# All loads of weights and of the first batch's mask rows issued by SyncE, and another order of the work

## The chip, the cores and the metric

One Trainium2 chip, one core of it. The metric is device time in microseconds of one execution, as the median of repeated runs; a profile is one more execution, taken with the hardware profiler.

## The reference

Cluster attention, then two feed-forward blocks, everything in float32 except that the weights arrive as float64:

```python
# q, k, v: (B=2, H=8, S=768, D=64); 16 centroids per head
q_assign = np.argmax(np.einsum('bhsd,hcd->bhsc', q_n, c_n), axis=-1)
k_assign = np.argmax(np.einsum('bhsd,hcd->bhsc', k_n, c_n), axis=-1)
mask = q_assign[:, :, :, None] == k_assign[:, :, None, :]
scores = scale * np.matmul(q, k.transpose(0, 1, 3, 2))
scores = np.where(mask, scores, -1000000000.0)
attn = softmax(scores)
x = (attn @ v), as (1536 tokens, 512)
h = x @ w_in                      # 512 x 2048
g = where(h >= 1, h, where(h <= -1, 0, (h + 1) ** 2 / 4))
x = g @ w_out                     # 2048 x 512
h = (x @ w1) * (x @ w2) @ w3      # 512 x 1024, 512 x 1024, 1024 x 1024
return h @ w_out2                 # 1024 x 512
```

## The kernel before

The work is cut into some three thousand small steps, each with a name, an engine, what it needs and which buffers it takes and frees (`add`, `Plan`). The steps run in an order that is written out: the string `ORDER` holds, two letters a step, the step's number and which of its engines does it (`Plan.order`). Engines run their own steps in that order, and wait for each other by semaphores. A DMA is a step of the engine that issues it, in that engine's line of work: "DMA" is SyncE (SP), which does nothing else; ScalarE (ACT) issues DMAs between its activations.

The stages, in the order of time. **Batch 0's attention** (to about 190 us): q, k of a pair of heads are split into a high and a low part by conversions on ACT or DVE (L352 and L354, tiles `k`, `q`, `kq`), L859 makes the scores of 128 queries in `sc`, L867 on VectorE takes the row maximum, L872 on GpSimd scales it, L880 on ACT makes the exponentials, L897 transposes them on TensorE, L968 multiplies by v. Beside it the float64 weights are loaded (`chunk`, load at L1101 into a `w` tile of 512 KB), turned into float32 by L1107 and L1111 on ACT and L1115 and L1121 on DVE, and stored to DRAM (`wd`, L1126) for later; L1169 multiplies w3 by w_out2 beforehand, and its results go through DRAM (`wp`). **Batch 1's attention beside batch 0's feed-forward** (190 to 470 us): the exponentials go through a float16 pair in `phl` (two buffers; L352 or L354 the high part, L357 the low), and SP transposes them by DMA (L927, `pt<-phl`, 46 times); the feed-forward's matmuls are L1239 with weights in `whl`. **Batch 1's feed-forward** (470 us to the end): a seven-product scheme of block matmuls (L1492, L1239) with sums on DVE and GpSimd (L1403, L357).

A weight that has been stored is loaded again into one of four `wf` buffers (L1103 in `chunk`, L1413 in `w_unit`), split into `whl` by L352 or L354 and L357, and used by the matmuls. A float64 load takes one of five `w` buffers at first, later of three, and waits for the L1121 that frees it. In batch 0 the mask rows of each head are copied from a tile `mask` into `kq` by two DMAs of `kq_fill` (L728). All these loads, 152 of weights and 14 of mask rows, stand in ACT's line of work. SP issues the loads of q, k, v, the stores, the transposes and the output. The framework tells DMAs' landings by eight semaphores, taken in turn by the DMAs of both engines in the order of the steps: a DMA waits for the one eight before it.

The mask copies' engine is chosen by the batch, and the weight loads name ACT outright:

```python
    def dma_of(b):
        return nc.sync.dma_start if b else nc.scalar.dma_start
```

Of the kernel before, what the change touches and what calls it, by code (L numbers as in the profile page):

```python
# [13 lines left out]
U32 = mybir.dt.uint32  # L14
# [29 lines left out]
    ",(,4,6&E,*<8<6<F<:<V+|<J<L+e<s<<&I<N%@&K<?,8,:,,,.<@+m,#,%<g,<,0,2,>,L,@,B,D+g,N,P<w=*,X,Z,]&N<e<i,F,R<k<Z<]"
    "<n<`<a<p=:;|<0<2,_,T,H,J,V&>+i+l,a,u,w,y<u<y<|=.=J=#%(,c&P-(-*-,+o<B<Q<R,|-#,e,g=>=,=<=0+q=X&@-.&B-4-6-8=@=B"
    "&M=2=D=i-%-:=5=6+s<q=%=(-0-2-<-@&c-B-D=N=L=P=R&S=U=V=Z=]=_&T=y->>0=k-F-L-X-Z-]-N,m,i=a,l-P=m=o=q=s=d=e>@-R-_"
    ">P=|>#>2&Y-H-u-w,o-e-g>%-J>a,q=8=G=H>(,s>4-a-T-V.(.*-d&Z>6-y=g=v=w>o-|>*>-&b>8>:%*>D&i&V&_>T&k&v>B>F>H&^>K>M"
    "&e.#.%-m-i.4.6.,..?#>s.@-k>e.0.3&o.8.B&m.D&g-o>.>=>>.:?4>R>V>c>q&s.L.N.P.X.<>X>Z.Z%B?(-q>N.F>g>i.R.>?F>u>l>w"
    "?%?*>z?,.H>n>~.T.]._.a.J?V.u.V-s>]/(/4?.?0/*/,.c?i&z(&?@>_/@/B.w?2?B?D&w($(-%,?8&q?y.m?Z?J/.?6?H?X&|((%D/6.y"
    ".|/#/8/:/<?m/%?:?<?>?L?]/D?N?_?k?o?a(..e/0/2?q/>%.%0%2%4%F?P.g?R/F?s/L/N/H/P?c@,@2@#@B?|%6%H/J(*/R@T?T?e?g%J"  # L50
    "%L/X%8%:%</Z.i.k.o?u@%@(@6@4@8/T0(/V/]/_.q.s@:?w@.@0@e/a/c/u@*0*0,@D@F@<@w@X/w@>0./y/|@i@V@g@N%N0406@H@J@L@Z"
    "/m/e@]00%P%R%T@kA.@`@m@o0#0%@|02080:@@@P@b@yA#A%@R@q0@0<0L0>/g/i0XA@AP/k0N0P0B0DA:/o0u0w0yA)@c@s@u0Z0R0F0T/q"
    "0H0KA*A2A0A40|0W0]0_0e0gA6ADAcABA,A<A>0a0cA8As/s1((0(2ARATAFAHAJ1*1,1.1#Ag(4(61416AVAXAe1%AMAiAkA]AZ0mAuAnAp"
    "100i1X1Z12B%Aw0kB,0o181:1@1L(:1N1P1B1D(=(8(>ANA_AaAy(AA|B#1R0q1<1]1T1>1F(B1_B/(E(H(M1e1g(NAqB(B*1H1J1V1a1d0s"
    "1i1kBJ2*2,(F(J2.Bi2022C.B01u1w1y1|(Z(P24(R1m(TBMBO1o2#2%26(V(X2(1q1sB2B4282:2<B6CLCkBkBn2FB82H2>2AD02B2DB>BP"
    "B]B@BBBDC02J2L2O2PC2B:B<BRCNCQB_BbBTBF2T2V2X2ZBHC4C6FLC82]BVD>2cBcBY2eB[2R2_2aBoBq2g2i2kBtC:C<BfBgC>B|C#C&Bu"
    "FPBw2m2oCn3%C@CB3(D2C(CD3*3,CF3436By383.30Fe3:CHCpCKC_CRCT3B3<(_C+CaCWC,3>(hD53D(]32CX3F3@CcCe(bFiD@(c(eG#DL"
    "DZ3H3K2y3P3R3TD#D%CZC]D(3V3LD*3NChCqCs3Y3Z3]CuD,DBD6D:3mD<DOCwD9DQD^Cz3_(jDiG(3a3c3e2qE.3gELD`2s3o(t3q3sDDDG"
# [1699 lines left out]
```

## Time and profile before

| what | us |
|---|---|
| median of 3 runs | 721.11 (721.01 to 721.91) |
| the profiled execution | 723.58 |
| its span, first to last instruction | 721.5 |
| busy in the span: PE, DVE, ACT, POOL | 699.0, 618.2, 468.2, 290.9 |
| mean share of full TensorE clock | 0.998 |

The span is the stretch between the first and the last instruction; the rest of the profiled execution lies around it. Busy time of an engine leaves out what its sequencer does: waiting, and issuing DMAs.

### The profile page before, as it was taken

What the parts mean: (1) busy time and instruction counts of PE and PEld (TensorE: products, weight loads), DVE (VectorE), ACT (ScalarE), POOL (GpSimd) and SP (SyncE); (2) the same over time, 40 slices, a digit from 0 to 9 for tenths busy, and PEclk for the clock granted to TensorE, in tenths of its full rate; (3) what the DMA queues carried; (4) which work ended last, traced back from release to release, by engine and by line L of the source; (5) the groups of instructions that cost most, each with busy time, mean ns of one, the idle gap of its engine ahead of it and who ended that gap; (6) DMA issues with size and microseconds to landing.
All of it is one profiled execution on the core that took longest, in us unless ns stands there. A gap on an engine that the chain in (4) does not pass through costs nothing.

```text
span 721.5 us, 11974 instructions
## 1 busy us (share of the span) xinstructions
PE 699.0 (97%) x4173; PEld 631.2 (87%) x4173; DVE 618.2 (86%) x1080; ACT 468.2 (65%) x872; POOL 290.9 (40%) x359
## 2 busy tenths in 40 slices
PE   5999999999999999999999989999999999999998
PEld 2876776677799999999899988999999999999997
DVE  7999999989889998898999879568878869999940
ACT  7998999779786877977787656236764525543211
POOL 3344433221253454455321312317573426387510
PEclk9999999999999999999999999999999999999999
DMA  8357867777989998998989898673222122121122
GB/s 313 124 179 232 278 208 251 249 250 219 231 190 199 216 226 220 215 243 160 267 216 247 208 155 202 155 219 113 59 88 74 45 73 61 52 80 59 58 70 77
DMA packets 125644, 122.36 MB, mean 170 GB/s; under 512 B 83792, under 2 KB 92432, under 8 KB 125584
## 3 DMA queue, kind: packets, MB, share of 16 engines
q1 hardware_dynamic: 103024, 62.18, 36.2%
q10 hardware_dynamic: 22560, 59.42, 26.3%
q8 instruction: 33, 0.54, 0.3%
q14 instruction: 27, 0.22, 0.1%
HBM read 75.79 MB, written 22.28 MB: 136 GB/s over the span
## 4 chain that ended last, share of the span: by engine, by line
PE 71%; DVE 11%; DMA 7%; ACT 6%; issue 3%; POOL 1%; ACTq 0%; SPq 0%; DVEq 0%; POOLq 0%
PE mo L1239 33%; PE sc L1239 6%; PE sc L859 6%; PE sc L1492 6%; PE mo L1492 4%; PE mo L1169 3%; PE av L976 3%; PE sc L897 2%; PE av L968 2%; DMA pt<-phl 2%; PE av L1239 2%; DMA wf<-wp 2%; PE av L1492 1%; DVE tv L1403 1%; ACT P L880 1%
## 5 line engine op out<-in xcount | busy, mean ns | idle before, releaser
L1239 PE MATMUL mo<-X,whl 128*128 128x384 f32 x912 | 167.9, 338 | 0.0
L1239 PEld LDWEIGHTS mo<-X,whl 128*128 128x128 f32 x912 | 159.5, 189 | 1.7 <-DVE G L354 0.3
L1239 PE MATMUL mo<-G,whl 128*128 128x384 f32 x672 | 124.1, 339 | 0.0
L357 POOL TENSOR_TENSOR whl<-wf,whl 128x512 fp32r<-128x512 f32 x62 | 81.2, 1310 | 97.9 <-DVE whl L354 42.2
L1239 PEld LDWEIGHTS mo<-G,whl 128*128 128x128 f32 x672 | 118.2, 188 | 1.0 <-issue 0.6
L867 DVE TENSOR_REDUCE nm<-sc 128x1 f32<-128x768 f32 x96 | 90.0, 950 | 5.7 <-PE sc L859 5.2
L872 POOL TENSOR_SCALAR nm<-nm 128x1 f32<-128x1 f32 x96 | 34.6, 360 | 146.9 <-DVE nm L867 141.5
L352 ACT ACTIVATE whl<-wf 128x512 fp32r<-128x512 f32 x71 | 44.4, 627 | 46.0 <-PE mo L1239 26.2
L1111 ACT ACTIVATE w<-w,down 128x512 uint32<-128x512 uint32 x72 | 54.5, 763 | 8.4 <-DMA pt<-phl 3.9
L859 PE MATMUL sc<-k,q 128*128 128x512 f32 (+1 forms) x192 | 54.1, 363 | 5.7 <-DVE phl L357 2.6
L880 ACT ACTIVATE sc<-sc,nm 128x768 f32<-128x768 f32 x46 | 40.0, 870 | 20.6 <-POOL nm L872 19.8
L1115 DVE SCALAR_TENSOR_TENSOR wf<-wf,w 128x512 uint32<-128x512 uint32 x72 | 51.0, 714 | 2.3 <-ACT wf L1107 1.7
L1107 ACT ACTIVATE wf<-w 128x512 f32<-128x512 f32 x72 | 47.4, 671 | 6.3 <-POOL whl L357 3.6
L1121 DVE SCALAR_TENSOR_TENSOR wf<-w,wf 128x512 uint32<-128x512 uint32 x72 | 50.3, 702 | 1.1
L880 ACT ACTIVATE P<-sc,nm 128x768 f32<-128x768 f32 x50 | 44.8, 898 | 9.9 <-DVE nm L867 5.6
L859 PE MATMUL sc<-kq 80*128 80x512 f32 (+1 forms) x192 | 49.7, 341 | 0.0
L357 DVE TENSOR_TENSOR phl<-sc,phl 128x768 f16<-128x768 f32 x46 | 43.8, 952 | 3.2 <-ACT phl L352 2.6
L357 DVE TENSOR_TENSOR whl<-wf,whl 128x512 fp32r<-128x512 f32 x50 | 35.1, 704 | 10.1 <-ACT whl L352 9.4
L859 PEld LDWEIGHTS sc<-k,q 128*128 128x128 f32 x192 | 31.4, 190 | 13.5 <-ACT pt L352 4.2
L897 PEld LDWEIGHTS sc<-ident,P 128*128 128x128 f32 x300 | 33.5, 140 | 10.1 <-ACT P L880 7.2
L1239 PE MATMUL sc<-G,whl 128*128 128x384 f32 x228 | 42.0, 339 | 0.0
L897 PE MATMUL sc<-ident,P 128*128 128x128 f32 x300 | 39.7, 275 | 2.3 <-ACT P L880 2.1
(235 smaller groups left out, 1462.0 us busy)
## 6 DMA issues: line engine op xcount, KB each, us to landing
wf<-wd ACTq DMA_DIRECT2D x64, 256.0 KB, 2.8
w<-in_w_out_dram ACTq DMA_DIRECT2D x24, 512.0 KB, 4.2
wd<-wf SPq DMA_DIRECT2D x48, 256.0 KB, 3.4
...
```

Of the source, the lines that this page charges most:

```text
L352: nc.scalar.activation(out=out, in_=in_, func=AF.Copy)
L357: (nc.gpsimd if e == "POOL" else nc.vector).tensor_tensor(out=out, in0=a, in1=b, op=ALU.subtract)
L859: nc.tensor.matmul(ps[:, n], q[0:n_rows, q0:q0 + 128], k[0:n_rows, n], start=first, stop=not first)
L867: nc.vector.tensor_reduce(out=nm, in_=T[("sc", b), s], axis=AX.X, op=ALU.max, negate=True)
L880: nc.scalar.activation(out=new(("P", b), s).rearrange("p n s -> p (n s)") if by_pe(s) else T[("sc", b), s], in_=T[("sc", b), s], func=AF.E ...
L897: nc.tensor.transpose(T[("sc", b), s][:, c], p[:, c], ident)
L1107: nc.scalar.activation(out=T["wf", i], in_=T[w64, i].bitcast(F32)[:, :, 1], func=AF.Abs, scale=float(2.0 ** -112))
L1111: nc.scalar.activation(out=lo, in_=lo, func=AF.Identity, scale=float(2.0 ** -29 - 2.0 ** -41), bias=down)
L1115: nc.vector.scalar_tensor_tensor(out=w, in0=w, scalar=3, in1=T[w64, i][:, :, 0], op0=ALU.logical_shift_left, op1=ALU.bitwise_or)
L1121: nc.vector.scalar_tensor_tensor(out=w, in0=T[w64, i][:, :, 1], scalar=0x80000000, in1=w, op0=ALU.bitwise_and, op1=ALU.bitwise_or)
L1239: nc.tensor.matmul(acc, w[:, a, k4 * 128:(k4 + 1) * 128], rhs(c, k4), start=(first and k4 == 0 and n == 0), stop=(last and k4 == 3 and n = ...
L1492: nc.tensor.matmul(ps, lhs(av, a, k), rhs(bv, c, k), start=k == 0 and n == 0, stop=k == 1 and n == 2,)
```

## The change

The steps that load weights, and those that copy batch 0's mask rows, are now steps of SP. What each loads, and where it lands, stays. `ORDER` is another string of the same steps; in it some steps that can run on two engines stand on the other one. The diff, of `ORDER` its first line:

```diff
-    "###*#,#0#%#(#8$V%X%[#.#2#4$0$.$6$2$X%e%h$8$:#F%V%b$<%c%q%k%m$Z$_$a%i%]$>$c$4$H#D$J#R#g%y&,:m:|%_#Z$%$(;0;>$@"
+    "###%#*#,#0#.#(#8#<$V%X%[$.%e%i$0%c%q#2#4$6%h%m$8$:$2$X#T#F#Z%V%b$_$<%_$a%y&,$Z$4#_$H#D$>$@$c$J%]$e$L%k$B$g$N"
...
-    def dma_of(b):
-        return nc.sync.dma_start if b else nc.scalar.dma_start
+    def dma_of(e):
+        return nc.sync.dma_start if e == "DMA" else nc.scalar.dma_start
...
-            dma = dma_of(b)
+            dma = dma_of(e)
...
-                    ("k2", u, h), {"DMA": 1.95} if b else {"ACT": 0.3}, p - 6.0, kq_fill(u, h),
+                    ("k2", u, h), {"DMA": 1.95} if b else {"DMA": 0.9}, p - 6.0, kq_fill(u, h),
...
-                nc.scalar.dma_start(out=new(w64, i), in_=src.bitcast(U32).rearrange("p (n t) -> p n t", t=2))
+                (nc.sync if e == "DMA" else nc.scalar).dma_start(out=new(w64, i), in_=src.bitcast(U32).rearrange("p (n t) -> p n t", t=2))
             else:
-                nc.scalar.dma_start(out=new("wf", i), in_=src)
+                (nc.sync if e == "DMA" else nc.scalar).dma_start(out=new("wf", i), in_=src)
...
-            add(("wl", i), {"ACT": 0.2}, t - 14.0, load, list(needs) + W_AFTER[i:i + 1], [(w64, i)], behind="w64", moves=((0.46, 1.8),))
+            add(("wl", i), {"DMA": 0.5}, t - 14.0, load, list(needs) + W_AFTER[i:i + 1], [(w64, i)], behind="w64", moves=((0.46, 1.8),))
...
-            add(("wl", i), {"ACT": 0.2}, t - 12.0, load, needs, [("wf", i)], behind="wf", moves=((0.46, 1.05),))
+            add(("wl", i), {"DMA": 0.5}, t - 12.0, load, needs, [("wf", i)], behind="wf", moves=((0.46, 1.05),))
...
-                nc.scalar.dma_start(out=new("wf", i), in_=wd[n])
-
-            add(("wl", i), {"ACT": 0.2}, t - 16.0, load, [("wd", n)], [("wf", i)], behind="wf", moves=((0.46, 1.05),))
+                (nc.sync if e == "DMA" else nc.scalar).dma_start(out=new("wf", i), in_=wd[n])
+
+            add(("wl", i), {"DMA": 0.5}, t - 16.0, load, [("wd", n)], [("wf", i)], behind="wf", moves=((0.46, 1.05),))
```

What this moves is shown at three places, where a name's number tells a buffer.

**SP, about 415 to 445 us**, in the last third of batch 1's attention: DMA transposes `pt<-phl`, stores `wd<-wf` and `xd<-tmp`. Before:

```order
L927 DMA_TRANSPOSE pt_97<-phl_112 128x12x128
L1017 DMA xd<-tmp 128x384
L927 DMA_TRANSPOSE pt_98<-phl_111 128x12x128
L1126 DMA wd<-wf 128x512
L927 DMA_TRANSPOSE pt_98<-phl_112 128x12x128
L1126 DMA wd<-wf 128x512 x2
L927 DMA_TRANSPOSE pt_96<-phl_111 128x12x128
```

and now, with the loads `w<-in_w_dram` among them:

```order
L927 DMA_TRANSPOSE pt_97<-phl_112 128x12x128
L1017 DMA xd<-tmp 128x384
L1101 DMA w_115<-in_w_dram 128x1024
L1126 DMA wd<-wf 128x512
L927 DMA_TRANSPOSE pt_98<-phl_111 128x12x128
L927 DMA_TRANSPOSE pt_98<-phl_112 128x12x128
L1101 DMA w_113<-in_w_dram 128x1024
L1126 DMA wd<-wf 128x512
L1101 DMA w_114<-in_w_dram 128x1024
L1126 DMA wd<-wf 128x512
L927 DMA_TRANSPOSE pt_96<-phl_111 128x12x128
```

Three loads that stood in ACT's line stand between the transposes, and two of them ahead of the transpose into `pt_96`.

**ACT, from its first mask (`mask_118`, L588) to its first exponential (L880)**, about 15 to 24 us; `w` and `wf` are weights on their way to float32. Before:

```order
L588 ACTIVATE kq_105<-sc_175,nbig 16x384
L728 DMA kq_106<-mask_118 16x2x384 x2
L1107 ACTIVATE wf<-w_114 128x512
L352 ACTIVATE vn<-sc_175 128x768
L1101 DMA w_117<-in_w3T_dram 128x1024
L1111 ACTIVATE w_114<-w_114,down 128x512
```

and now:

```order
L588 ACTIVATE kq_105<-sc_180,nbig 16x384
L1111 ACTIVATE w_113<-w_113,down 128x512
L1107 ACTIVATE wf<-w_114 128x512
L588 ACTIVATE mask_118<-sc_180,nbig 128x384
L352 ACTIVATE vn<-sc_180 128x768
L1111 ACTIVATE w_114<-w_114,down 128x512
L1107 ACTIVATE wf<-w_115 128x512
L1107 ACTIVATE wf<-w_116 128x512
L1111 ACTIVATE w_115<-w_115,down 128x512
```

The mask copies and the load are gone from between the activations, and one more L1107 stands ahead of the first exponential.

**ACT, about 72 to 78 us**, where q and k of a later pair of heads are split. Before:

```order
L1101 DMA w_113<-in_w_out_dram 128x1024
L352 ACTIVATE kq_105<-kq_119 64x768
L1107 ACTIVATE wf<-w_115 128x512
L728 DMA kq_107<-mask_118 16x2x384 x2
L352 ACTIVATE pt_98<-sc_174 128x768
```

and now:

```order
L352 ACTIVATE kq_105<-kq_119 64x768 x2
L1107 ACTIVATE wf<-w_115 128x512
L352 ACTIVATE pt_98<-sc_179 128x768
L352 ACTIVATE whl<-wf 128x512
L1111 ACTIVATE w_117<-w_117,down 128x512
```

One conversion more stands on ACT here, and one less on DVE. Over the program, of batch 0's conversions into `k`, `kq` and `q` ACT has 26 (20 before) and DVE 10 (16 before); GpSimd has four operations fewer than before, of all its work.

## Rows read from the trace of the kernel before

**Rows 1.** The page, part 1: busy us, share of the span, instructions.
```profile
PE 699.0 (97%) x4173; PEld 631.2 (87%) x4173; DVE 618.2 (86%) x1080; ACT 468.2 (65%) x872; POOL 290.9 (40%) x359
```

**Rows 2.** Busy time by stretches: length, busy us (instructions) of each engine, PEclk, DMA, GB/s.
```profile
20.00:50.00 30.00, 28.59 (x192) 23.18 (x191) 28.83 (x47) 28.51 (x51) 11.96 (x18) 1.00 0.45 144
50.00:100.00 50.00, 49.22 (x298) 36.48 (x298) 47.37 (x78) 46.21 (x79) 21.70 (x25) 1.00 0.74 245
100.00:150.00 50.00, 47.68 (x293) 33.21 (x290) 47.02 (x73) 44.55 (x78) 15.56 (x21) 1.00 0.75 246
150.00:200.00 50.00, 48.44 (x279) 37.31 (x278) 45.63 (x72) 39.29 (x70) 11.20 (x22) 1.00 0.84 233
200.00:400.00 200.00, 199.52 (x1242) 187.88 (x1242) 184.44 (x298) 154.18 (x282) 83.88 (x102) 1.00 0.93 218
400.00:470.00 70.00, 67.84 (x422) 63.37 (x417) 53.65 (x88) 33.68 (x61) 19.53 (x25) 0.98 0.81 175
470.00:600.00 130.00, 130.00 (x742) 129.59 (x741) 103.91 (x216) 66.98 (x145) 63.18 (x70) 1.00 0.32 98
600.00:640.00 40.00, 39.01 (x220) 38.35 (x220) 39.03 (x75) 19.96 (x46) 21.64 (x24) 1.00 0.18 53
640.00:685.00 45.00, 44.01 (x247) 42.64 (x247) 43.59 (x89) 14.64 (x36) 32.68 (x39) 1.00 0.21 65
```

**Rows 3.** Timeline of ACT, 56 to 63 us: start, us, engine (ACTq issues), what.
```profile
56.22 0.90 ACT L880 ACTIVATE P<-sc,nm 128x768 f32<-128x768 f32 x1
56.23 0.33 ACTq L1101 DMA_DIRECT2D w<-in_w_in_dram  x1
...
62.79 0.60 ACTq L728 DMA_DIRECT2D kq<-mask  x1
```

**Rows 4.** Chain of waits, 15 to 27 us: start, us, what.
```profile
18.85 0.16 ACTq L728
...
25.56 0.19 ACTq L1101
```

**Rows 5.** Groups: ACT 20:200 us, DVE 50:100, DVE whole; busy us, mean ns | idle before.
```profile
L1107 ACT ACTIVATE wf<-w 128x512 f32<-128x512 f32 x39 | 25.4, 676 | 1.6 <-DMA wd<-wf 1.2 <-issue 0.3
L352 ACT ACTIVATE kq<-kq 64x768 fp32r<-64x768 f32 x5 | 4.2, 841 | 0.1
...
L354 DVE CAST kq<-kq 64x768 fp32r<-64x768 f32 x4 | 2.2, 552 | 0.1
...
L357 DVE TENSOR_TENSOR whl<-wf,whl 128x512 fp32r<-128x512 f32 x50 | 35.1, 704 | 10.1 <-ACT whl L352 9.4
```

**Rows 6.** Chain of waits, 405 to 445 us.
```profile
417.98 12.90 DMA pt<-phl
```

**Rows 7.** Timelines of DVE, ACT, PE, 425 to 436 us; in brackets idle before, releaser.
```profile
430.97 0.96 DVE L354 CAST phl<-sc 128x768 f16<-128x768 f32 x1 [4.22 <-DMA pt<-phl]
...
426.79 4.50 ACTq L1101 DMA_DIRECT2D w<-in_w_dram  x2
431.33 0.75 ACT L1111 ACTIVATE w<-w,down 128x512 uint32<-128x512 uint32 x1 [3.92 <-DMA pt<-phl]
...
432.97 1.01 PE L859 MATMUL sc<-k,q 128*128 128x512 f32 x2 [2.16 <-DVE phl L357]
```

**Rows 8.** Busy time by stretches, columns as in rows 2.
```profile
433.00:437.00 4.00, 4.00 (x15) 3.81 (x16) 3.62 (x6) 2.29 (x5) 1.23 (x2) 0.61 0.89 299
```

**Rows 9.** Landing of the transposes L927: all 46, then those of 415 to 435 us.
```profile
DMA to landing us min/median/max: 3.6/4.2/13.0
...
DMA to landing us min/median/max: 3.7/10.3/13.0
```

**Rows 10.** ACT's timeline, 238 to 262 us: a load, and the split of what it brought.
```profile
240.11 0.33 ACTq L1103 DMA_DIRECT2D wf<-wd  x1
...
251.80 0.63 ACT L352 ACTIVATE whl<-wf 128x512 fp32r<-128x512 f32 x1
```

**Rows 11.** SP's waits ahead of transposes L927, 200 to 400 us: ns min/median/max, first and last start.
```profile
L927 SPq EVENT_SEMAPHORE  x34: 17/17/4611, 201.4 to 396.0; - x34
```

More of the change, by code (lines that the diff above doesn't have):

```diff
@@ L44 @@
[L44 to L58, printed above, removed]
@@ new lines @@
+    "&4*m<%;u+@+#+&+B+<*i*l+0+2+L+N+X;w;X<H<X+D+F+P+R;Z&*+T+H<c&G+Z*o<**r<,<.+>;z&><s+]+_+u+a+e&/&<+g+J+V+d*s,4+w"
+    ",(,*<6<8,6<:<F<J&8<V&I%(<L<<<N&E+y+|<Z;i,,,.+m,8<?<@,:<w,#,%,0,<,2,>&J,@,L,B,D,N,P<g,X,Z,]<]<`<b=*=:<e;k,F,R"
+    ";|<0,_%%=J<2<i<k<n<o=X,T,H,J,V+i+l,a,u,w,y<u<y=.,c<|-(-*=#+o<B<Q=i<R&P,|=N-,=,&@&B,e=0=<=>-.-4-#-6&c+r+s-8,g"
+    "-:=2=5=y&N=7=@=B=D-%=]<q-0-2=L=P-<=%=m=R=Z&R=T-@-B=_-X-L-N->-D-F&L=V>0=k>@-P,i,k&T%@=a-Z-]=(>P=d=e-R&i&u-_>4"
+    "&Z>#,m,o,r-H-u-w=o-K=8=G=q=H=s-a.(.*,s=|>%>D>(&a>a>o>2-T-V-c-y-e-g-|&k&W&_=g=u&e.4.,.#.%-m.6>6=w>8>:&p>+>B&X"
@@ new lines @@
+    ">F>H>-&]>K>L-i-l...0.@.3.B-o?#&s?4%B>T>s&g.8.:>.>=>>.<>R>V>X>c?(>e.L.N>g>q-q.X&m.>>N.D.F.P.R.T?%.Z.]._.H.J.V"
+    "?F%*>Z>u>i?V?*>w>l>y?,.a&q.u.c>]>n?/?0>~-s/4/(/*/,&z&|(&?@/@&w?6?J?8?i.w.y/B>_(.?2?B?D?Z(#(-%,/.()%D.m?m?H?X"
+    ".|/#/6/8/:/</0?:?<?>?k/%/2/>?y@2?]?L?o?_?N?P?c.e.g?q%.%0%2%4%F/D/F/L/N/H%H?R?T@B@#/J?s?a@T@,@6/P/R?u%6%8?e?g"
+    "%:%<@e%J%L/T.i.k/X/Z.o/V?|@%@4@8?w@.@0@(@*@:/]/_/a.q.s@F/c@D@X@<@>0(/u0*/w/y0406%N/|@wA.(*@H0,0./m@J@V@L@N%P"
+    "%R/e%T000#@Z@g@i@k080:@|0%02A@@]@`@a@m@o@y@@@P@q@RA#AP(40<0@0L0>A:0N0X/g/i/k0B0u0Z0P0R0D0FA%A(0w0]0_A*0yA2/o"
@@ new lines @@
+    "/qADA0AB@c@s@uAcAs0T0H0K0WA40a0cAT0|AFAHA,A<A>0e0gA6/sARAV1((0(2(61*1,AKA8AXAZ1#141%AM1618Ag1.0mAeAiAkAnAoA]"
+    "AwAuB,10121X1ZB%0i0k0o1L1@1N1BAN1:1<(:(=A_AyA|(8(>AaB#1P1R1T(A1>(D(C(M1D1F1]1_1e1g(N0qAqB(B*1H1a1J1V1d1iBJ(H"
+    "0s(F(ZBi2*2,B.B02.201u1w1y1|(P(R2324BL1k1m1o1r1s(T(VC.(JBNBlBm2#2%2(26(X282:CLCkB2D0B4B7B8B;B>B@2<BBBD2F2H2J"
+    "B=2>2@2BC0C32D2L2NB]B_BP2P2RFLD>2T2VBaBFBRBcBHCNBTBVCQBe2XC4C62c2eBYB[2Z2]2_2aBoBqC8C:C=BsBu2gBg2i2kDLB|C#3%"
+    "3(3*2m2oCmC&C?BxByC(3,C@CBCDCFC_3436D2D4C*CoCa3.30(]CcDZCeCg383:3<32CRCTDACICjCKDi2q3>3@Cq3B3DC-CVCX3FFeD#G#"
@@ new lines @@
+    "D%D)3H3J2s3P3R3T3V3L3NDND*DCC[CsCuDQCwFPE.2y3_D,D:3Y3Z3]Fi(aD63aD.(_3c3m3o(c(eC]3e3gD=(jD83i3kD]DD3qDF3s(s(k"
+    "DHDJ(h3u3w3|D_(uELDVDX2u2wDkDRDTCy(o2|4#3y(mDm404244E046483#4>(w4@4B4%4)(qE3EkF04DDeDaENDgEP4:4<4G4HF>C|D|4L"
+    "4N4PE#DcE%FN)(FRFTDo4JFVEnEoDqDsE(E+Du4RE,4U4V4X4ZE@4]EBEEDwDyFgEFFkEIFmFoE4E6E8E:4_E_EaEd4aEK4*5:GLE<E>4c4e"
+    "EeG(F2F5Gu4g(y(|)#)%4,4.G%EgG*G,HDEiERF@F#F%F)ETEVGP5<5>EX5@F*FBEqEsEvFYFZ4i4k4m5BGN5D5FG.F6F8GRGyGwEwG|E[GT"
+    "H#H%F,F:F<Fq4o4qHHHm4w4y4|4s4uFHF/FDFs5#G1G3FJF])*HF5%HJ5(5H5JGVI,5*FFF_HLIDHoEyFa5VHq5L5N5P5,Hs5RGXG@GBGEHu"
@@ new lines @@
+    "Hw5TFcHN5X5ZG[FuGFE]).),5e5gFw5])5FyF|5`5a5cE|)1)25iI.5.I0I2IHH(I4I]IuGIGJG]G_GaGiGk5kGcGm5s5u5nGoGfH*5oG450"
+    "52G6G8G:5wGgHPHSHyI6IF5y5|G=545658IJ6#IL6(6*G>H|5qI_GqGsH8H:IaJDIcIyH<H>)6Iw6%)AI|H,H.H0H2INJ#J%6,6.HTHVHXH4"
+    "60)9IeI8I:)<HaHc6R6THZ62HeI(I*H7IPHg)BJmISI#6V6X6ZJFJH64);)>IjIkHjK46D6]6FHAJJI%JL66I<I>KTIgHCI@6H6JJ(H]6a6c"
+    "JqJoJsJu)DIX6L6N6_6e6g6iKuIT6PHk6k6mJPJRKXIBK6JNIZJ+)FK868K:IVK<6>)HJw)J)LK>6o6q6s7#Im7%H`Io7(KVKZK]6u6w6y6|"
+    "K_)NL<LTJTJVJYJZKwJ,J.J0J2IqJzJ|72Is74767*KyJ]J_J4J7K|7,7.J8J:J<J>JAK@70KCL#6:Ja7N787:7<7>JcJf6<6@7PJgJjJlJB"
@@ new lines @@
+    "KDKFKIKJ7RL@K#K%KaL>Kc7]7_7TK(K*LB7VKLKN7a7cKPLV7e7@7XK,K.LD7gL(L*KeKgLXK0Lu)P7Z7iLyLwKRLZKiLHL]L|7k7m7o7H6B"
+    "L%M4L_MTM#K27y7|LJLF)TKk7q7sL,L.KmMm7u7w8#8%L1L2M%8(8*8,Lb8<8>M8L4L6M(KoKqKsL8L:)VLL7B8@8BM6M:MV8.M<M>LN7D7F"
+    "807JLcLPLeMXMZMqMoM]M*LSM,M@)_N482NLLg)S)]8486)X88LmMb)cLi8DM.MBMD)hMs)a)e8F7L8:LoM_LlMdMu)[8HN6NmNNMLM08JMF"
+    "8X8Z8]M2MNMyM~MHMKMeN8N:8g8i8kMPMi8_8aNPLqLsMhN<8c8LNR8m8oN@NT8qN,N>)iMSNB8e8sNYNZ)k)mMwN#8R9*9,9.N%O,OLMkNq"
+    "N.NH)o)q)sNoNsN)NuNV9092N0N*8uNe948w8yNyN~NJ96O0O.NgNjOPNDO2O4NF988N8PN39:9<O9NlOeP,O:8|9#ONO#O%Nw9%9(OROTN]"
@@ L96 @@
+    "f#fifgf%hHf(gwgyh&g|fmh*gVgLgFgXhhh$fofqfZfkgTgJh<hJfshjh.h3gZh,hoh>hLi(h7h0hqfufwgPgagNg_hBhNg]giglh8h(hsgc"
+    "gmh4hmi+i,h@hFhDhkhThXhPhRgfgghVh_i.i0hZh]hui2i4hbhch|i6i>i8iDiNiaiFiHiPi#idhxi@ifiLiJiihyiSiTigi%iWiBi:i<ik"
+    "iXiniZi]i_ioiqisiuiwiyi|"
 )
```

64 lines of the change are left out of this document (23 added, 41 removed).

## The prediction

> **What bounds the kernel now.** Begin with the page's busy times: TensorE is busy for 699.0 of the span's 721.5 us [rows 1]. What the change can win is therefore inside 22.5 us of idle TensorE time, plus what a lowered clock costs. Neither the matmuls nor their number change. Next read the busy times by stretches for where those 22.5 us lie [rows 2]. From 20 to 200 us TensorE lacks 1.41, 0.78, 2.32 and 1.56 us, 6.07 together, and there VectorE is busy for 28.83 + 47.37 + 47.02 + 45.63 = 168.85 of 180 us, ScalarE for 158.56. From 200 to 400 us it lacks 0.48, from 400 to 470 us 2.16, from 470 to 600 us nothing, from 600 to 640 and from 640 to 685 us 0.99 each, with VectorE busy for 39.03 of 40 and 43.59 of 45. The remaining 12 are the first 20 us, when there is nothing to multiply, and the tail. So three places can be argued about: the attention of batch 0, where VectorE and ScalarE together set the pace; one hole between 400 and 470 us; and the VectorE-bound stretch from 600 us.
>
> Then the chain of waits. Its one large link that a DMA makes is at 417.98 us: a transpose that takes 12.90 us to land [rows 6]. The timelines after it show what hangs on it [rows 7]: VectorE's next `phl` conversion (L354) waits 4.22 us for it, ScalarE's L1111 at 431.33 idles 3.92, and TensorE's scores 2.16, which is all that TensorE lacks in that stretch. After this hole the granted clock from 433 to 437 us is 0.61 [rows 8], between its levels of 2.4 and 1.2 GHz.
>
> **The change, part by part.** The sum is made against the profiled execution: 723.58, of which 721.5 are the span. It lies 2.47 above the median of 721.11, so the sum's differences are taken from the median at the end.
>
> *ScalarE's issuing.* 166 DMA issues leave ScalarE. A load's issue takes 0.33 us, a mask copy's 0.60 [rows 3]: 152 x 0.33 + 14 x 0.60 = 58.6 us. That looks like a tenth of ScalarE's 468.2, but it lies beside work: the load issued at 56.23 runs under an exponential that began at 56.22 and ends at 57.12 [rows 3]; the sequencer issues while the engine computes. On the chain of waits from 15 to 27 us, where ScalarE has most to do, three such issues of about 0.2 us stand, the first 0.16 and the last 0.19 [rows 4]. They go, about 0.5 us. In return one more L1107 stands ahead of the first exponential, 0.68 us [rows 5]. Both ends: 0.5 gained, or 0.7 - 0.2 = 0.5 lost; I take **0**.
>
> *Conversions from VectorE to ScalarE in batch 0.* Six more of the 36 conversions of q and k are on ScalarE: 0.84 us each there, 0.55 on VectorE [rows 5]. VectorE loses 6 x 0.55 = 3.3 us, ScalarE gains 6 x 0.84 = 5.0. Upper end: the two engines hold up all that TensorE lacks there, and better balance gives back all 6.07. Lower end: ScalarE gets the whole 5.0 us in its busiest stretch, 50 to 100 us, where it is busy for 46.21 of 50 [rows 2]: 51.2 us of work in 50, 1.2 lost. VectorE has 180 - 168.85 = 11.15 us idle and yet TensorE waits, so its load is only part of the cause. I take the nearest measured thing, the waits in the two busier VectorE stretches, 20 to 100 us, 1.41 + 0.78 = 2.19, and halve it as VectorE is one of two engines that set the pace: **1.0 gained**.
>
> *The hole at 418 to 437 us.* The two loads that ScalarE issues at 426.79 take its sequencer 4.50 us, and L1111 stands behind them [rows 7]; the transpose of 417.98 travels beside weight loads. In the changed order ScalarE has no load to wait with, so 3.92 us of idle ScalarE go. Whether TensorE gains depends on the transpose itself: those between 415 and 435 us take 10.3 us in the middle, all 46 take 4.2 [rows 9]. If its loads go one after another in SP's line, at most one or two of them share the DMA engines with a transpose, and it lands nearer 4.2 than 12.9; `phl` is free 8.7 us earlier, and the 4.22 us of VectorE wait go, with the 2.16 of TensorE. At 0.61 granted clock four microseconds do the work of 2.44, so the fall costs 4 x 0.39 = 1.56. Upper end: 2.16 + 1.56 = 3.7. Lower end: the same stall moves, 0 gained. I take **3.0**, nearer to the upper end, because only transposes in that stretch are so slow.
>
> *From 600 us.* GpSimd has four operations fewer. If VectorE takes all four between 600 and 685 us, at the 0.70 us of its L357 [rows 5], it has 2.8 us more to do, where 0.97 + 1.41 = 2.38 are free [rows 2]: 0.4 lost at worst. At best TensorE's 0.99 + 0.99 = 2.0 close. The order moves as much to as away from VectorE, so **0**. From 470 to 600 us VectorE is busy for 103.91 of 130 and covers any such change; without that cover each operation would cost its 0.7.
>
> *SP's line.* It takes 166 more DMAs. At ScalarE's prices these are 58.6 us. SP computes nothing, so only order matters: each DMA waits for the one ahead of it in line. A load is issued 11.7 us before the split of what it brought (240.11, 251.80) [rows 10], so a load that stands behind one transpose (4.2 us) is still in time. For transposes it is the other way: a load that waits for a free `w` holds them. SP's waits ahead of a transpose are now 17 ns in the middle and 4.61 us at most [rows 11]. Best: no loss (0). Worst: it costs as much as the present hole, 3.7 us, at two places in batch 1's attention: 7.4 lost. I take **0**, since the middle wait is nothing.
>
> Sum: 0 + 1.0 + 3.0 + 0 + 0 = 4.0 us. The profiled execution would be about 719.6 (span 717.5), the median 721.1 - 4.0 = **717.1**.
>
> **The rivals.** *No change (721).* The hole of 418 us only moves. For it: transposes travel on SP's queue already, and the DMA engines are busy for 0.93 of 200 to 400 us [rows 2]; the same bytes through one queue are the same load. Then the 3.0 go, the balance gives 0 to 1: 720.1 to 721.1. The Trainium skill, page DMA: Bandwidth & Descriptors, section Issuing engines are not separate DMA queues, says that all engines' DMAs end on the same 16 DMA engines, and that issuing from several saves only the time of issuing. By that rule alone this rival is what comes. The trace agrees as to the share of issuing in the chain (0.2 us a time), but shows transposes between 3.6 and 13.0 us, which the rule does not speak of.
>
> *Slower: transposes behind waiting loads (727.5).* In the new order two loads into `w` stand ahead of the transpose into `pt_96`. Each needs a `w` that L1121 has freed. ScalarE's line shows what such a wait is: 4.50 us for two issues at 426.79 [rows 7]. Now it would stand on SP, and the transpose, both `phl` buffers, VectorE's next conversion and TensorE's scores stand behind it, in this order. From 4 us on (the 4.22 that VectorE waited cost TensorE 2.16) it decides. Two such places cost 2 x 3.7 = 7.4, less the 1.0 of the balance: 721.1 + 6.4 = 727.5. For it: that stretch has no spare buffer for `phl`. Against it: an order can put loads behind the L1121 that frees their buffer, and TensorE lacks only 0.48 us in the 200 us before, while SP already waits up to 4.61 there [rows 2, 11]. The Trainium skill says on the same page, section Anatomy of one DMA, that DMA engines do not wait on semaphores; the issuing sequencer does, before it dispatches. By that rule a load that waits holds all that is behind it on SP; the 4.50 us agree.
>
> *Larger gain (710).* If the balance gives all 6.07 and the hole all 3.7, and from 600 us half of 2.0 comes back: 10.8, so 710.3. For it: VectorE is above 94% in 20 to 150 us. Against it: VectorE is relieved by 3.3 us only.
>
> **How the numbers follow.** Forecast (717.1): 0.40. No change: 0.15. Slower: 0.27. Larger gain: 0.18. The sum's bounds alone reach from 0.5 + 6.1 + 3.7 + 2.0 = 12.3 gained (708.8) to 0.5 + 1.2 + 0 + 0.4 + 7.4 = 9.5 lost (730.6). The range takes both rivals with a little beyond each, **709 to 729**, and leaves out less than 2 in 10; the forecast's own range is 714.5 to 719.5. A measurement here tells about 0.2%, 1.4 us, from no change: faster by more is 0.40 + 0.18 = 0.58, within it 0.15, slower 0.27.
>
> **What would show it.** Right: no link of over 6 us from a transpose in the chain around 418 us; the stretch 400 to 470 us with TensorE over 69 of 70 and a granted clock of 1.00; VectorE's sum in 20 to 200 us lower by about 3, ScalarE's higher by about 5, and TensorE's lack there about 5. The balance is wrong if ScalarE's exponentials start later at 24 us, or if TensorE waits longer for ScalarE's `pt` or `P` from 50 to 100 us. The slower rival shows as semaphore waits over 4 us on SP ahead of L1101 with a transpose behind, VectorE waiting there for `pt<-phl`, and a clock under 1.00 after it. If TensorE's idle time between 20 and 200 us shrinks to 2 or less, the larger gain is right.

## The result, and the profile after

| | before | after |
|---|---|---|
| median, us | 721.18 (4 runs, 721.01 to 721.91) | 714.70 (4 runs, 713.85 to 715.5) |
| the profiled execution, and its span | 723.58, 721.5 | 714.0, 712.3 |
| ratio of the times | | 0.9908, 95% interval 0.9891 to 0.9925 |

The change is faster by 6.5 us; 717.1 had been forecast. Busy time by stretches of the new kernel (length, then busy us and instructions of PE, PEld, DVE, ACT and POOL, granted clock, DMA share, GB/s), beside [rows 2, 8]:

```profile
0.00:20.00 20.00, 13.57 (x81) 7.86 (x82) 14.82 (x37) 15.93 (x22) 7.02 (x15) 1.00 0.91 329
20.00:50.00 30.00, 28.03 (x185) 22.14 (x184) 27.11 (x44) 28.38 (x50) 11.94 (x18) 1.00 0.43 136
50.00:100.00 50.00, 48.82 (x293) 36.16 (x293) 45.30 (x71) 48.40 (x84) 20.80 (x26) 1.00 0.69 229
100.00:150.00 50.00, 48.24 (x296) 32.92 (x294) 47.11 (x73) 45.53 (x78) 15.55 (x21) 1.00 0.77 252
150.00:200.00 50.00, 49.33 (x291) 39.35 (x290) 45.67 (x72) 40.01 (x71) 17.23 (x26) 1.00 0.80 231
200.00:400.00 200.00, 199.99 (x1249) 187.92 (x1248) 180.21 (x288) 155.65 (x282) 84.59 (x103) 1.00 0.89 219
400.00:470.00 70.00, 70.00 (x438) 66.52 (x437) 54.62 (x94) 35.60 (x65) 18.70 (x23) 1.00 0.79 198
470.00:600.00 130.00, 130.00 (x741) 129.69 (x740) 112.63 (x234) 69.05 (x151) 57.55 (x68) 1.00 0.27 85
600.00:640.00 40.00, 40.00 (x230) 40.00 (x229) 37.67 (x80) 18.15 (x43) 19.87 (x24) 1.00 0.20 60
640.00:685.00 45.00, 45.00 (x258) 44.85 (x257) 40.43 (x86) 14.33 (x34) 26.35 (x32) 1.00 0.23 71
```

What TensorE lacks in each stretch, as length less busy time:

| us | before | after | |
|---|---|---|---|
| 0 to 20 | 8.25 | 6.43 | -1.8 |
| 20 to 200 | 6.07 | 5.58 | -0.5 |
| 200 to 400 | 0.48 | 0.01 | -0.5 |
| 400 to 470 | 2.16 | 0 | -2.2 |
| 600 to 685 | 1.98 | 0 | -2.0 |
| the rest | 3.6 | 3.8 | +0.2 |

That is 6.7 us of idle time. TensorE's busy time falls by another 2.5 (699.0 to 696.5), 1.56 of it, by the prediction's estimate, in the stretch at a granted clock of 0.61 [rows 8], which is gone. Together they are the 9.2 us between the two spans. The medians differ by less, since the profiled execution of before lay 2.4 us above its median and that of after 0.7 below.

The first two rows of the table are not firm. Three runs below keep the old order and the old queue up to 190 us (the tail, the 12 loads, the later loads on SP): in their profiles TensorE lacks 7.6 to 8.4 us to 20 us and 5.1 to 5.5 from 20 to 200. The new kernel, profiled again, lacks 7.9 and 5.5. So the 0.5 from 20 to 200 us is no gain, and the 1.8 of the first 20 us is not there in every execution.

The page's part 1, and the queue (packets, MB, share of 16 engines), say that all went to one queue and the bytes stayed (62.18 and 59.42 MB on two queues before):

```profile
PE 696.5 (98%) x4172; PEld 630.6 (89%) x4173; DVE 608.6 (85%) x1076; ACT 474.5 (67%) x880; POOL 281.1 (39%) x355
...
q1 hardware_dynamic: 125584, 121.60, 61.0%
```

The landing of all 46 transposes, beside [rows 9], and what hung on it: the chain of waits from 400 to 450 us is TensorE's matmuls alone.

```profile
DMA to landing us min/median/max: 3.6/4.1/8.1
```

```profile
by line: PE mo L1239 80.2%; PE sc L859 12.6%; PE av L976 6.1%; PE mo L954 1.3%
```

How long SP waits is told by the view of its waits, not by how long its semaphore instructions take, as [rows 11] have it: a DMA's own wait is not in those. From 190 to 470 us, ahead of transposes (the longest group) and of weight loads (us in total, times, longest):

```profile
SPq L927 <- DVE wf L1115: 22.3, 5, 7.8
...
SPq L1101 <- DVE wf L1121: 6.2, 6, 2.2
```

What a transpose waits for is its own `phl`: of the 46, the one in the middle leaves 0.03 us after VectorE's L357 has written it (in the kernel before too). The latest leaves 3.7 us after it (before: 1.9), as it stands on SP behind a load that waits for a `w`:

```profile
316.26 0.95 DVE L357 TENSOR_TENSOR phl<-sc,phl 128x768 f16<-128x768 f32 x1
```

```profile
317.37 3.03 SPq L1101 DMA_DIRECT2D w<-in_w_out_dram  x2
...
320.94 2.06 SPq L927 DMA_TRANSPOSE pt<-phl  x1
```

It cost TensorE nothing: from 200 to 400 us it lacks 0.01.

### The profile page after: what moved, and what is told of

Same layout as the page of the kernel before. It is cut to its first block, busy times and chain, and to the rows that moved or that the text cites. A ratio compares the mean times of both kernels' runs of the same rounds, so it can differ in the third digit from the quotient of the medians.

```text
span 712.3 us, 12067 instructions
## 1 busy us (share of the span) xinstructions
PE 696.5 (98%) x4172; PEld 630.6 (89%) x4173; DVE 608.6 (85%) x1076; ACT 474.5 (67%) x880; POOL 281.1 (39%) x355
## 4 chain that ended last, share of the span: by engine, by line
PE 86%; ACT 9%; issue 2%; DVE 2%; DMA 1%; SPq 0%; ACTq 0%; POOL 0%; DVEq 0%
PE mo L1239 40%; PE sc L1492 9%; PE sc L859 8%; PE sc L1239 6%; PE mo L1492 5%; PE av L976 3%; PE mo L1169 3%; PE sc L897 3%; PE av L968 2%; PE av L1492 2%; ACT P L880 2%; ACT pt L352 2%; ACT w L1111 2%; PE av L1239 1%; ACT wf L1107 1%
## 5 line engine op out<-in xcount | busy, mean ns | idle before, releaser
L357 POOL TENSOR_TENSOR whl<-wf,whl 128x512 fp32r<-128x512 f32 x65 | 86.3, 1329 | 125.9 <-DVE whl L354 64.6
L1239 PE MATMUL mo<-G,whl 128*128 128x384 f32 x720 | 133.6, 339 | 0.0
L1239 PEld LDWEIGHTS mo<-G,whl 128*128 128x128 f32 x720 | 126.4, 188 | 1.2 <-issue 0.3
L872 POOL TENSOR_SCALAR nm<-nm 128x1 f32<-128x1 f32 x96 | 30.6, 318 | 131.3 <-DVE nm L867 125.4
L352 ACT ACTIVATE whl<-wf 128x512 fp32r<-128x512 f32 x74 | 46.2, 627 | 38.9 <-PE mo L1239 15.3
L357 POOL TENSOR_TENSOR wh<-ws,wh 128x256 fp32r<-128x256 f32 x47 | 36.1, 782 | 41.0 <-ACT wh L352 26.3
L880 ACT ACTIVATE sc<-sc,nm 128x768 f32<-128x768 f32 x46 | 39.9, 867 | 17.8 <-POOL nm L872 17.5
L1121 DVE SCALAR_TENSOR_TENSOR wf<-w,wf 128x512 uint32<-128x512 uint32 x72 | 50.5, 707 | 1.1
L1107 ACT ACTIVATE wf<-w 128x512 f32<-128x512 f32 x72 | 47.6, 672 | 4.1 <-DMA wd<-wf 2.1
L880 ACT ACTIVATE P<-sc,nm 128x768 f32<-128x768 f32 x50 | 44.6, 895 | 6.9 <-POOL nm L872 3.8
L357 DVE TENSOR_TENSOR phl<-sc,phl 128x768 f16<-128x768 f32 x46 | 43.8, 952 | 5.6 <-ACT phl L352 5.2
L352 ACT ACTIVATE pt<-sc 128x768 f32<-128x768 f32 (+1 forms) x43 | 33.7, 808 | 5.2 <-PE sc L897 3.8
```

The lines of the kernel that those rows point to most:

```text
L352: nc.scalar.activation(out=out, in_=in_, func=AF.Copy)
L357: (nc.gpsimd if e == "POOL" else nc.vector).tensor_tensor(out=out, in0=a, in1=b, op=ALU.subtract)
L880: nc.scalar.activation(out=new(("P", b), s).rearrange("p n s -> p (n s)") if by_pe(s) else T[("sc", b), s], in_=T[("sc", b), s], func=AF.E ...
L1107: nc.scalar.activation(out=T["wf", i], in_=T[w64, i].bitcast(F32)[:, :, 1], func=AF.Abs, scale=float(2.0 ** -112))
L1121: nc.vector.scalar_tensor_tensor(out=w, in0=T[w64, i][:, :, 1], scalar=0x80000000, in1=w, op0=ALU.bitwise_and, op1=ALU.bitwise_or)
L1239: nc.tensor.matmul(acc, w[:, a, k4 * 128:(k4 + 1) * 128], rhs(c, k4), start=(first and k4 == 0 and n == 0), stop=(last and k4 == 3 and n = ...
```

## The experiments

Each was timed in interleaved rounds with the kernel before on the same chip. Three chips were used (runs 1 to 4, 5 to 8, 9 to 12); before's median on them was 721.3, 720.5 and 720.8.

**The new order alone.** The new kernel, loads and copies issued by ScalarE:

```diff
-        return nc.sync.dma_start if e == "DMA" else nc.scalar.dma_start
+        return nc.scalar.dma_start
...
-                (nc.sync if e == "DMA" else nc.scalar).dma_start(out=new(w64, i), in_=src.bitcast(U32).rearrange("p (n t) -> p n t", t=2))
+                nc.scalar.dma_start(out=new(w64, i), in_=src.bitcast(U32).rearrange("p (n t) -> p n t", t=2))
```

(and so for the other two loads). The first line of this edit also puts on ScalarE the 24 copies of batch 1 that SP issues in both kernels, which the expectation does not say; so only batch 0 is read from it.

> The new order, but all loads and mask copies issued by ScalarE again, at their places in that order. If the gain of 6.5 us comes from the order alone (theory O): 714 to 716, ratio 0.990 to 0.993. If it comes from the loads leaving ScalarE's line (theory Q): 719 to 722, with ScalarE waiting for transposes or stores ahead of its loads between 400 and 470 us. If an order made for SP holds ScalarE up at loads that wait for a free w: over 724.

783.37 us, ratio 1.086 (1.082 to 1.090). The third case came, and far beyond its bound. In batch 0 alone TensorE lacks 17.85 us from 20 to 200 us (after: 5.58), with VectorE and ScalarE busy for only 144.70 and 145.30 us, and the granted clock is 0.93:

```profile
20.00:200.00 180.00, 162.15 (x923) 119.85 (x925) 144.70 (x219) 145.30 (x248) 56.02 (x76) 0.93 0.60 200
```

**The old order with all loads on SP.**

```diff
-        return nc.sync.dma_start if b else nc.scalar.dma_start
+        return nc.sync.dma_start
...
-                nc.scalar.dma_start(out=new("wf", i), in_=src)
+                nc.sync.dma_start(out=new("wf", i), in_=src)
```

> The old order, but all loads and mask copies issued by SP. Theory Q: 715 to 718, TensorE without a gap between 400 and 470 us (2.16 before) and a granted clock of 1.00 there. Theory O: 720 to 722, the hole of 418 us stays. If loads that wait for a free w hold the transposes behind them (the slower rival): over 724, with SP waiting over 4 us at loads L1101 and VectorE waiting for pt<-phl.

728.3 us, ratio 1.0098 (1.0064 to 1.0132): slower by 7. The hole is closed as theory Q says, and yet the time is that of the third case. By stretches, of the fastest of its six executions (724.86 us, mean granted clock 0.998; the others have 0.997 to 0.990), so that the trace shows only half of the 7 us:

```profile
0.00:20.00 20.00, 10.53 (x54) 4.51 (x55) 12.85 (x32) 14.27 (x19) 7.01 (x15) 0.96 0.76 283
...
400.00:470.00 70.00, 70.00 (x455) 65.08 (x453) 57.03 (x95) 36.34 (x66) 20.88 (x28) 1.00 0.81 196
...
640.00:685.00 45.00, 42.79 (x238) 41.11 (x238) 43.19 (x85) 14.69 (x36) 32.14 (x39) 1.00 0.23 73
```

The loss begins in SP's timeline: four weight loads stand ahead of a load of q. SP issues it at 8.96 us, when an earlier load of k has landed (8.94), and it lands 9.00 us later (chain of waits). In the kernel before it leaves at 4.75 us and lands 5.0 us earlier. TensorE waits for it:

```profile
4.58 3.76 SPq L1101 DMA_DIRECT2D w<-in_w_out_dram  x4
8.96 0.33 SPq L513 DMA_DIRECT2D kq<-in_qT_dram  x1
```

```profile
2.66 6.28 DMA kq<-in_kT_dram
8.94 0.02 issue
8.96 9.00 DMA kq<-in_qT_dram
```

```profile
18.00 1.25 PE L539 MATMUL sc<-kq,cT 128*32 128x384 f32 x6 [1.91 <-DMA kq<-in_qT_dram]
```

So a line that holds others up behind it is real, but its victims are loads of q and mask copies in batch 0 (another 1.9 us of TensorE's wait is for `kq<-mask`), not transposes: these took at most 5.9 us here.

**The tail and the start of the new order on the kernel before.** Loads stay on ScalarE. The edits of `ORDER` are given in words, here and below.

```diff
-ORDER = (the 3036 steps of before)
+ORDER = (the first 2600 steps of before, then the others as they follow in the new order)
```

> The kernel before with its loads on ScalarE, and from step 2600 of 3036 on (about 600 us) the order and the engine choices of the new kernel. If TensorE's 2.0 us between 600 and 685 us went by the order of that stretch alone: 719.2, with at most 0.3 us of idle TensorE there. If they need the loads on SP: 721, with 1 to 2 us of idle TensorE left.

719.96 us, ratio 0.9977 (0.9952 to 1.0002). By the time unclear, by the trace nearly what was expected: TensorE lacks 0.07 and 0.44 us where it lacked 0.99 and 0.99:

```profile
600.00:640.00 40.00, 39.93 (x228) 39.60 (x227) 36.90 (x79) 18.44 (x43) 19.29 (x24) 1.00 0.16 47
640.00:685.00 45.00, 44.56 (x250) 43.34 (x249) 41.99 (x89) 15.46 (x39) 28.62 (x36) 1.00 0.19 59
```

```diff
-ORDER = (the 3036 steps of before)
+ORDER = (the first 200 steps of the new order, then the others as they follow in before)
```

> The kernel before with its loads on ScalarE, and the first 200 steps (to about 40 us) in the order of the new kernel. If the 1.8 us that TensorE wins in the first 20 us come from that order: 719.4, TensorE busy for 13 to 14 of the first 20 us. If they come from SP's line, where weight loads go behind those of q and k: 721, TensorE busy for about 11.8 of them.

733.15 us, ratio 1.015 (1.012 to 1.019), slower by 11, which neither case had. TensorE is busy for 11.96 of the first 20 us, as the second case says: without SP's line the new order wins nothing there. Most of the loss comes behind it, at a granted clock of 0.77, whose price is, by an estimate, 30 x 0.23 = 6.9 us:

```profile
20.00:50.00 30.00, 23.61 (x128) 20.78 (x129) 16.18 (x27) 19.37 (x33) 6.26 (x9) 0.77 0.36 123
```

ScalarE's timeline shows why (start, us; the kernel's lines are one lower here):

```profile
23.88 0.58 ACT L587 ACTIVATE mask<-sc,nbig 128x384 fp32r<-128x384 f32 x1 [1.46 <-PE sc L579]
23.89 0.82 ACTq L1100 DMA_DIRECT2D w<-in_w_out_dram  x2
...
27.54 0.68 ACT L1106 ACTIVATE wf<-w 128x512 f32<-128x512 f32 x1 [1.73 <-DMA w<-in_w_out_dram]
...
32.39 0.73 ACTq L727 DMA_DIRECT2D kq<-mask  x1
```

The loads stand in ScalarE's line behind the mask of 23.88, which waits for TensorE; they leave at 23.89, and the L1106 behind them waits for what they bring. In the new kernel the same two loads leave SP from 8.70 us on (8.70, 1.29 us, x2 in its timeline). The first mask copy leaves at 32.39.

**Two loads of k exchanged.** SP's line reads `L513 DMA kq<-in_kT_dram x3` in both kernels, but before loads k of the second pair of heads ahead of that of the first.

```diff
-ORDER = (..., load k of pair 1, load k of pair 0, ...)
+ORDER = (..., load k of pair 0, load k of pair 1, ...)
```

> The kernel before with two of SP's first loads exchanged: k of the first pair of heads is loaded ahead of k of the second, as in the new order. If TensorE's later start (first scores against the centroids at 8.25 us before, 7.25 after) comes from the place of that load in SP's line: TensorE starts these at 7.0 to 7.4 us and the time falls by about 1.0 us, ratio 0.9986. If the lead is lost again in the ScalarE-bound stretch that follows: same start, no change in time.

720.69 us, ratio 0.9998 (0.9971 to 1.0025). TensorE's first scores begin 1.2 us earlier than the 8.25 of before,

```profile
7.05 1.51 PE L539 MATMUL sc<-kq,cT 128*32 128x384 f32 x8 [0.96 <-DVE cT L450]
```

and it is busy for 12.75 us of the first 20 (11.75 before). In the three runs with the old start these scores begin at 7.63 to 8.02 us, and TensorE is busy for 11.63 to 12.38, so the lead is 0.6 to 1.2 us. A gain of 1.0 us, 0.0014, lies inside the interval, as does none.

**Only the loads beside the hole on SP**, in the old order (12 loads, 401 to 460 us):

```diff
-                nc.scalar.dma_start(out=new("wf", i), in_=src)
+                (nc.sync if i in HOLE else nc.scalar).dma_start(out=new("wf", i), in_=src)
```

(and so for the other two loads; `HOLE` holds the numbers 82 to 93).

> The kernel before, only the 12 loads that ScalarE issues between 401 and 460 us issued by SP, at the same places of the old order. If the stall of 417 to 437 us comes from loads that stand in a second queue beside the transposes: no transpose over 9 us, TensorE busy for 70.0 of 70 us and a granted clock of 1.00 from 400 to 470 us, time lower by 3 to 4 us, ratio 0.995. If the stall is of the old order itself: 67.8 of 70 us, clock 0.98, no change. If loads that wait for a free w hold up the transposes behind them on SP: slower by 2 us or more.

718.79 us, ratio 0.997 (0.995 to 0.9991): the hole is closed, for 1.7 to 2.2 us and not 3 to 4.

```profile
400.00:470.00 70.00, 70.00 (x438) 66.54 (x437) 53.09 (x89) 32.86 (x60) 18.90 (x24) 1.00 0.76 188
```

The run before it, where these loads are still ScalarE's, shows on the same chip what was there to be won: TensorE lacks 2.24 us, but the granted clock of the stretch is 1.00, so the price of the clock was not paid there.

```profile
400.00:470.00 70.00, 67.76 (x422) 64.19 (x421) 51.43 (x86) 31.11 (x57) 18.34 (x23) 1.00 0.81 178
```

What the DMA engines did from 417 to 433 us, in before and then in this run (all queues, then each):

```profile
DMA packets 5043, 2.75 MB, mean 172 GB/s; under 512 B 4504, under 2 KB 4632, under 8 KB 5042
...
q1 hardware_dynamic: 4728, 1.58, 94.1%
q10 hardware_dynamic: 314, 1.15, 27.8%
...
pt<-phl SPq DMA_TRANSPOSE x3, 12.9
```

```profile
DMA packets 5609, 3.50 MB, mean 219 GB/s; under 512 B 4800, under 2 KB 4888, under 8 KB 5607
...
q1 hardware_dynamic: 5607, 3.47, 97.5%
...
pt<-phl SPq DMA_TRANSPOSE x3, 5.2
```

With two queues the same 16 engines moved 172 GB/s, with one 219. The rate by itself shows no stall: in the last run below, with two queues and none, it is 165 in the same window.

**The pieces together** on the kernel before: the two k loads, the 12 loads, the tail (the edits above).

> The three pieces together on the kernel before: the two first k loads exchanged, the 12 loads of 401 to 460 us on SP, and from step 2600 on the order of the new kernel. If these pieces are what the change gains (1.0 + 3.8 + 1.5 to 2.0): lower by 6.3 to 6.8, about 714.7, ratio 0.991, with 166 - 12 loads still on ScalarE until about 600 us. If the gain needs all loads off ScalarE: 717 to 719.

716.97 us, ratio 0.9947 (0.9926 to 0.9968): 3.8 of the 6.5 us, not all. Its profiled execution was the slowest of its 12 (721.81), so its stretches are not read. The other 2.7, with about 2 either way, lie in what the pieces leave out: the rest of the new order, with its loads on SP. No run takes them apart.

**Conversions back on VectorE**, in the new kernel: in `ORDER` the steps that split q and k in batch 0 take the engines they had before (12 steps differ, moved in either direction).

> The new kernel, with the conversions of q and k in batch 0 on the engines of the kernel before (some five to six back from ScalarE to VectorE), same order otherwise. By the prediction's step (VectorE's relief is worth 1.0): 715.7, TensorE's idle time between 20 and 200 us up from 5.6 to about 6.6. If the relief is worth nothing: 714.7. If it did harm, as ScalarE is then the busier one: 713.5 to 714.

717.95 us, ratio 0.9952 (0.9929 to 0.9976), against this:

**The new kernel again.** No edit.

> The new kernel unchanged, on the same chip as the runs beside it. About 714.7 and a ratio of 0.991 as in its first runs. Against the 717.95 with the conversions put back on VectorE: 716.9 if their move is worth the 1.0 us of the prediction, 714.8 if it is worth the 3.1 us of idle TensorE by which the two profiles differ from 20 to 200 us.

713.81 us, ratio 0.990 (0.9874 to 0.9925). From the ratios the conversions' move is worth 0.0052, 3.7 us, with about 2.5 either way (two intervals, two chips). From 20 to 200 us, first with the conversions on VectorE, then the new kernel:

```profile
20.00:200.00 180.00, 171.30 (x1037) 127.60 (x1038) 167.85 (x258) 154.71 (x268) 65.62 (x89) 1.00 0.69 216
```

```profile
20.00:200.00 180.00, 174.52 (x1060) 130.48 (x1059) 165.15 (x258) 162.20 (x279) 66.35 (x91) 1.00 0.70 220
```

TensorE gains 3.2 us where VectorE loses 2.7. Its waits for VectorE's `nm` and `pt` to 200 us are 2.0 and 1.6 us in the first, 0.6 together in the second.

**Only the mask copies of batch 0 back on ScalarE**, in the new kernel:

```diff
-            dma = dma_of(e)
+            dma = nc.sync.dma_start if b else nc.scalar.dma_start
```

> The new kernel with the 14 mask copies of batch 0 issued by ScalarE again, at the same places of the order; all loads stay on SP. If issuing lies beside ScalarE's work (14 x 0.6 = 8.4 us of its sequencer): no change against the new kernel, within 0.5 us. If ScalarE's line is what makes a DMA late: slower by 1 to 3 us, with TensorE waiting for kq<-mask.

720.47 us, ratio 0.9988 (0.997 to 1.0006). Fourteen DMAs of 0.6 us are worth 6.7 us against the 713.81 of the run beside it. In the new kernel, then in this run, the first of them:

```profile
17.40 1.42 SPq L728 DMA_DIRECT2D kq<-mask  x2
```

```profile
26.38 0.67 ACTq L728 DMA_DIRECT2D kq<-mask  x1
```

```profile
29.38 0.59 PE L859 MATMUL sc<-kq 80*128 80x512 f32 x2 [1.22 <-DMA kq<-mask]
```

The place in the order is the same. On ScalarE it stands behind activations, the first exponential among them, and the copy leaves 9 us later; the scores wait for it. This is a price in the new order alone: the kernel before, whose order has the copies earlier in ScalarE's line, issues the first at 18.29.

```profile
18.29 0.72 ACTq L728 DMA_DIRECT2D kq<-mask  x1
```

From 20 to 200 us TensorE lacks 8.93 us (the new kernel 5.48), and the clock is 0.99:

```profile
20.00:200.00 180.00, 171.07 (x1027) 126.05 (x1026) 160.74 (x250) 158.57 (x272) 62.61 (x87) 0.99 0.67 212
```

**Only the later loads on SP**, in the old order:

```diff
-                nc.scalar.dma_start(out=new("wf", i), in_=src)
+                (nc.scalar if i in EARLY else nc.sync).dma_start(out=new("wf", i), in_=src)
```

(and so for the other two loads; `EARLY` holds the numbers 0 to 43).

> The old order; the 44 loads before 190 us and the mask copies stay on ScalarE, the 108 later loads are SP's. If what the old order lost with all loads on SP (7 us) was lost in batch 0, where loads of q, k and masks stand behind weights: 717 to 719, the hole at 418 us closed, ratio 0.995. If it was lost later: 722 or more, with TensorE below 43.5 of 45 us from 640 to 685 us.

719.35 us, ratio 0.9971 (0.9955 to 0.9988). The two runs differ only in the engine of the early loads and of the mask copies. So the 7 us that the old order lost with all loads on SP, and the 1.5 more that it gained here, come from batch 0. Some stays: from 640 to 685 us TensorE is busy for 42.81 us, 1.2 less than before.

**The 12 loads beside the hole back on ScalarE**, in the new kernel:

```diff
-                (nc.sync if e == "DMA" else nc.scalar).dma_start(out=new("wf", i), in_=src)
+                (nc.scalar if i in HOLE else nc.sync).dma_start(out=new("wf", i), in_=src)
```

(and so for the other two loads).

> The new kernel with the 12 loads of 397 to 455 us issued by ScalarE again, at the same places of the new order. If a second queue beside the transposes makes the stall: transposes over 9 us, TensorE 67 to 69 of 70 us from 400 to 470 us, slower than the new kernel by 2 to 4 us. If the new order alone keeps the stall away: no change.

714.31 us, ratio 0.9909 (0.9886 to 0.9933), as the new kernel. The transposes from 400 to 460 us and the stretch:

```profile
DMA to landing us min/median/max: 3.7/4.3/6.4
```

```profile
400.00:470.00 70.00, 70.00 (x438) 66.51 (x437) 55.68 (x94) 35.39 (x64) 18.39 (x23) 1.00 0.79 192
```

So the new order has no hole with either queue, and in the old order the hole goes when these loads go to SP. What exactly makes the stall stays open. In the kernel before, two loads on ScalarE leave within 0.4 us of the transpose of 417.98. That alone does not make it: in the new order two loads also leave close ahead of a transpose (428.09, 429.12 and 429.66 us), and it lands after 6.0 us; and in the run with the new order's first 200 steps, old order and ScalarE's queue from there on, two loads leave at 430.74 and 431.10 us, the transpose at 431.16 lands after 8.2, and TensorE is busy for 70.00 of 70 us.

## Why the prediction was right, and where it was not

Sign and range held, and its signs came: no transpose in the chain around 418 us; TensorE at 70.0 of 70 us with a clock of 1.00 in the hole's stretch; VectorE down by 3.7 (168.85 to 165.2; about 3 had been named) and ScalarE up by 3.8 (about 5) from 20 to 200 us; TensorE's lack there 5.58 (about 5). But the terms were less right than their sum. The hole, 3.0 of the 4.0, came; the 1.0 of batch 0 did not show as a gain there; and the rest of the 6.5 us comes from places that the sum put at nothing.

*ScalarE's issuing (0, bounds 0.5 either way).* This step failed. Issuing does lie beside work, but it asked only what an issue takes of ScalarE's time, and not what stands ahead of the issue in ScalarE's line. With the new order's other steps in place, taking 14 mask copies off that line is worth 6.7 us. That is no part of the 6.5, but it is part of why the new order does not work from ScalarE. The Trainium skill, page DMA: Bandwidth & Descriptors, section Issuing engines are not separate DMA queues, which the rival "no change" rested on, says that issuing from several engines saves only the time of issuing. For this kernel the measurement decides against that as a price: a copy takes about 0.6 us to issue on either engine, and on ScalarE the first leaves 9 us later.

*Start.* Not priced at all: the prediction set the first 20 us aside as time "when there is nothing to multiply", but TensorE is busy for 11.75 of them. The exchange of two k loads, which the listing's names hide, moves TensorE's first scores from 8.25 to 7.25 us; its worth in the time stays unclear (0.9998).

*Conversions (1.0).* Right in sign, too small: 3.7 by the ratios, 3.2 by the trace. The halving "as VectorE is one of two engines that set the pace" failed. That the stretch as a whole gained nothing clear means that the rest of the change costs TensorE there about as much as the conversions give; what of it was not separated. From 20 to 100 us, where the term was read, TensorE lacks more than before, 3.15 after 2.19, and its waits for ScalarE's `pt` and `P` from 50 to 100 us, which were to show a wrong balance, rose from 0.6 to 1.0 us; from 100 to 200 us it lacks less, 2.43 after 3.88. The first exponential starts at 23.3 us as before.

*The hole (3.0).* Closed, and the chain ran as written: transpose, `phl`, VectorE, scores. In the two profiles it is 2.16 + 1.56; alone on another chip 1.7 to 2.2. The cause was half right: one queue closes it in the old order, but so does the new order with two. The fall of the clock does not come with every hole: in the run of the two k loads TensorE lacks 2.24 us there at 1.00.

*From 600 us (0).* Mis-sized: 2.0, its upper end. "The order moves as much to as away from VectorE" was wrong: VectorE's work from 600 to 685 us fell from 82.62 to 78.10 us, while from 470 to 600 us, where TensorE lacks nothing in either kernel, it rose from 103.91 to 112.63. The tail run shows 1.5 of it from the order alone.

*SP's line (0).* Right for the new order, but not for its reason, "the middle wait is nothing". SP does wait ahead of transposes, for what they copy; where transposes stand, a load waits at most 2.2 us for its `w`, and the one transpose that is 3.7 us late lies under the 4 us from which the prediction let it decide. The slower rival's price came from a wrong reading as well. The 4.50 us of two loads on ScalarE [rows 7] are no wait for a free `w`: the last L1121 before them ends at 426.75 us, and the second load leaves at 430.9, as the transpose of 417.98 lands (417.98 + 12.90 = 430.88), which [rows 7] name as what ended ScalarE's idle time. DMAs of both engines take the eight semaphores in turn, so a load on ScalarE can wait for a transpose on SP; that it was this turn fits the trace and was not tried.

```profile
426.06 0.69 DVE L1121 SCALAR_TENSOR_TENSOR wf<-w,wf 128x512 uint32<-128x512 uint32 x1
```

That this rival gave 6.4 us and the old order lost 7.0 is chance. SP's line does hold others up in an order that was not made for it, but its place is q and masks in batch 0, not transposes. The q load left at 8.96 us, behind four weight loads, where it left at 4.75 before; what the prediction cited beside this rival from the Trainium skill, page DMA: Bandwidth & Descriptors, section Anatomy of one DMA, agrees as far as the issue goes: SP holds the load back until 0.02 us after a load of k has landed. The 9.00 us to its landing are not SP's waiting.

The two halves of the change do not add: queue alone +7.0, order alone far slower (by batch 0 of its run), together -6.5. To price them one by one and add, as the prediction did, was luck as much as method.
